# A division moved behind the casts of the weights, and its DMA turn moved behind the last weight load

## The chip, the cores and the metric

One core of a Trainium2 chip. The metric is device time in microseconds (us) of one execution; lower is better. A profile covers one execution; its span is about 1.8 us shorter than that execution's time.

In the lines of the profile PE is TensorE (matmuls), PEld its weight loads, DVE VectorE, ACT ScalarE, POOL GpSimd and SPq the queue of SyncE; L365 is line 365 of the kernel. The granted clock is the share of TensorE's full clock that it was given. A load "lands" when its data is there. The "turn" is the transposing DMA of block 8, the "division" that block's three VectorE instructions (den, reciprocal, multiply).

## The reference

A linear attention with cosine reweighting (batch 8, 8 heads, 576 positions, head size 64) feeds a two-layer network with a gated activation. Cut to what matters:

```python
q_p, k_p = phi(q), phi(k)                  # relu, times cos and sin of the position
kv  = einsum('bhsf,bhsd->bhfd', k_p, v)
num = einsum('bhsf,bhfd->bhsd', q_p, kv)
den = einsum('bhsf,bhf->bhs', q_p, z)[..., None] + 1e-06     # z: sum of k_p over positions
x   = (num / den), heads side by side       # 4608 x 512
h   = x @ w_in                              # 512 x 2048
g   = h * sigmoid(beta * h)
out = g @ w_out                             # 2048 x 512
```

## The kernel before

The 4608 rows of x go through the network in nine chunks of 512 (eight blocks of 64 rows). The first chunk takes blocks 0 to 7 of batch 0; block 8, the last of that batch, is the first of the second chunk. The weights come as float32 through four staging buffers (w_in 0 to 3, then w_out 0 to 3 in the same buffers) and are cast to bfloat16. The order of instructions is written by hand. All the loads below are requested by SyncE, and in the trace of the kernel before they land in the order in which they are requested: raw v, k and q of batch 1 at 33.25, 36.25 and 39.23 us, the turn at 39.70, the halves of w_out 2 at 41.07 and 42.39, those of w_out 3 at 45.19 and 46.54.

```python
def cast_halves(i, fs=(0, 256)):            # each half: 3 casts on VectorE, 1 on GpSimd (i > 1)
    for f in fs:
        for gj in GJ:
            cast_win(i, gj, "pool" if i > 1 and gj == GJ[3] else "dve", f, f + 256)

def rest():                                 # program order behind column tile 4 of the first chunk
    cast_halves(2, (0,))
    x_mul(x_rden(2, 0, 8, NQ, (0, 1)), 8, NQ)      # block 8: den, reciprocal, multiply (VectorE)
    cast_halves(2, (256,))
    cast_halves(3)
    load_w("out", 0); load_w("out", 1)
    load_raw(1, "v"); load_raw(1, "k"); load_raw(1, "q")
    x_turn_dma(0, 8, 9)                            # block 8 turned by a DMA transpose into xt
    load_w("out", 2, 2); load_w("out", 3, 2)
    for j in range(8):
        cast_out(j)                                # w_out 0 and 1, scaled by 1/beta
    v_scale(1, 0); k_relu(1); q_relu(1, 0); q_relu(1, 1)
...
early = {
    4: lambda: (num_mm(8, 0, 2, 0), num_mm(8, 1, 2, 1), rest()),
    ...
    22: lambda: (kv_mm(1, 0, 6), kv_mm(1, 1, 6), kv_take((0, 1), 6, "act")),
    23: second,          # PE transposes q of batch 1; VectorE scales w_out tile 8
}
# slots 4 to 15: h_group(0, slot)              x @ w_in, column tile = slot      (line 365)
# slots 16 to 23: o_part, row tiles 0 to 7 of w_out;  24 to 31: row tiles 8 to 15 (line 390)
# then the second chunk, whose first tile reads block 8
```

## Time and profile before

| | before |
|---|---|
| time | 294.94 us, median of 3 runs (294.49 to 295.12) |
| span, granted clock | 292.5 us, 0.999 |
| PE busy | 285.7 us, 98% |
| part that the change touches | 22 to 51 us |

From the page of the kernel before, the busy tenths of PE and of the DMA engines in 40 slices of 7.3 us:

```profile
PE   8799999999999999999999999999999999999994
...
DMA  7999999999998099807990699139102810131033
```

PE is full nearly everywhere, but so are the DMA engines in nearly all of the first twelve slices.

SyncE's requests in the kernel before (start, length of the request on its queue, line, what):

```profile
24.48 0.51 SPq L78 DMA_DIRECT2D raw_q<-in_q_dram  x1
25.47 5.96 SPq L350 DMA_TRANSPOSE xt<-xs  x1
31.55 4.31 SPq L94 DMA_DIRECT2D w_stage<-in_moe_w_out_dram  x4
```

These are requests, not transfers: raw q, requested at 24.48, lands 14.75 us later, at 39.23. The stretch in which the queue serves the turn shows in the DMA engines' rate (stretch; then busy time and number of instructions of PE, weight loads, VectorE, ScalarE and GpSimd; clock, DMA share, GB/s):

```profile
36.00:37.00 1.00, 1.00 (x7) 0.45 (x5) 0.73 (x1) 1.00 (x3) 0.00 (x0) 1.00 1.05 385
37.00:38.00 1.00, 1.00 (x6) 0.43 (x5) 0.63 (x1) 0.04 (x1) 0.00 (x0) 1.00 1.83 254
38.00:39.00 1.00, 1.00 (x50) 0.68 (x52) 0.00 (x0) 0.00 (x0) 0.00 (x0) 1.00 0.38 80
39.00:40.00 1.00, 1.00 (x43) 0.67 (x32) 0.74 (x2) 0.03 (x1) 0.00 (x0) 1.00 0.94 299
```

### The profile page before, as it was taken

How to read it: one execution, taken by the hardware profiler on the slowest of the kernel's cores; microseconds unless marked ns; L12 is line 12 of the kernel's file. 1: busy time of each engine (PE TensorE's matmuls, PEld its weight loads, DVE VectorE, ACT ScalarE, POOL GpSimd, SP SyncE). 2: the span in 40 equal slices, each digit the busy share in tenths (PEclk: the TensorE clock that was granted, in tenths of full speed). 3: DMA queues.
4: the chain of work that ended last, by engine and by line, in shares of the span. 5: the costliest groups of instructions: out<-in, count | busy, mean ns of one | idle time of the engine just before them, and what ended most of it. 6: DMA issues, size and time to landing. Idle time of an engine off the chain costs nothing.

```text
span 292.5 us, 7217 instructions
## 1 busy us (share of the span) xinstructions
PE 285.7 (98%) x3072; PEld 143.2 (49%) x3072; DVE 114.2 (39%) x287; ACT 143.0 (49%) x228; POOL 74.5 (25%) x89
## 2 busy tenths in 40 slices
PE   8799999999999999999999999999999999999994
PEld 7454455455445544554445444454455444444444
DVE  5989876834900392029301950086005000000000
ACT  5777847862166315721473137412760277137511
POOL 1443000642380038202740255013601210000000
PEclk9999999999999999999999999999999999999999
DMA  7999999999998099807990699139102810131033
GB/s 247 376 391 386 392 312 390 301 249 330 178 284 311 2 173 270 351 6 137 240 394 24 128 235 395 37 67 204 36 2 55 140 36 0 39 83 23 0 74 72
DMA packets 50736, 53.89 MB, mean 184 GB/s; under 512 B 31232, under 2 KB 31632, under 8 KB 50704
## 3 DMA queue, kind: packets, MB, share of 16 engines
q1 hardware_dynamic: 47744, 45.95, 53.7%
q0 software_dynamic: 2688, 7.34, 9.7%
q8 instruction: 24, 0.39, 0.6%
q10 hardware_dynamic: 272, 0.14, 0.2%
q14 instruction: 8, 0.07, 0.1%
HBM read 36.71 MB, written 9.44 MB: 158 GB/s over the span
## 4 chain that ended last, share of the span: by engine, by line
PE 84%; DMA 9%; DVE 4%; issue 0%; SPq 0%
PE ps L390 39%; PE ps L365 38%; DMA w_stage<-in_moe_w_in_dram 4%; PE ps L280 3%; DMA w_stage<-in_moe_w_out_dram 3%; DVE win L108 3%; PE ps L259 2%; DMA raw_q<-in_q_dram 2%; PE ps L408 1%; DVE wout L116 1%; PE ps L339 0%; SPq L78 0%; DVE xs L302 0%; DVE o_sb L411 0%; DVE rden L295 0%
## 5 line engine op out<-in xcount | busy, mean ns | idle before, releaser
L365 PE MATMUL ps<-xt,win 128*128 128x512 bf16 (+1 forms) x580 | 127.7, 378 | 0.2 <-DVE win L108 0.2
L390 PE MATMUL ps<-wout,g_t 128*128 128x512 bf16 x560 | 124.4, 379 | 0.1
L372 ACT ACTIVATE g_t<-ps,beta 128x512 bf16<-128x512 f32 x144 | 98.6, 688 | 33.7 <-PE ps L365 33.7
L365 PEld LDWEIGHTS <-win 128*128 128x128 bf16 x580 | 56.0, 98 | 66.5 <-issue 0.6
L390 PEld LDWEIGHTS <-g_t 128*128 128x128 bf16 x560 | 53.9, 98 | 64.0 <-issue 0.6
L385 POOL DMA_DIRECT2D out_dram<-o_sb x56 | 35.9, 645 | 138.2 <-ACT o_sb L396 138.2
L396 ACT COPY o_sb<-ps 128x512 f32<-128x512 f32 x35 | 20.2, 588 | 98.2 <-PE ps L390 94.0
L271 DVE CAST kv<-ps 128x520 bf16<-128x520 f32 x6 | 4.2, 700 | 68.3 <-PE ps L259 68.3
L217 POOL TENSOR_TENSOR qs<-qt,tanr 128x1152 bf16<-128x1152 bf16 x12 | 28.4, 2384 | 7.0 <-DMA qt<-qb 7.0
L411 DVE COPY o_sb<-ps 128x256 f32<-128x256 f32 (+1 forms) x2 | 0.7, 358 | 62.7 <-PE ps L408 62.7
L302 DVE TENSOR_TENSOR xs<-ps,rden 128x768 bf16<-128x768 f32 (+4 forms) x26 | 22.8, 884 | 0.9 <-DVE rden L295 0.2
L214 DVE TENSOR_SCALAR vb<-raw_v,cos 128x256 bf16<-128x256 f32 x63 | 17.1, 346 | 0.2 <-DMA raw_v<-in_v_dram 0.2
L291 DVE TENSOR_TENSOR den<-ps,eps 128x12 f32<-128x12 f32 (+4 forms) x26 | 4.1, 158 | 33.5 <-PE ps L280 33.5
L214 DVE TENSOR_SCALAR vb<-raw_v,sin 128x256 bf16<-128x256 f32 x54 | 14.7, 345 | 0.0
L280 PEld LDWEIGHTS <-qt 64*64 64x64 bf16 x576 | 10.4, 106 | 4.9 <-issue 4.0
L280 PE MATMUL ps<-kv,qt 64*64 64x65 bf16 x576 | 11.7, 195 | 0.5 <-ACT kv L269 0.5
L189 DVE TENSOR_SCALAR qb<-raw_q 128x1152 bf16<-128x1152 f32 x16 | 11.4, 752 | 1.6 <-DMA raw_q<-in_q_dram 1.6
L280 PE MATMUL ps<-kv,qs 64*64 64x65 bf16 x576 | 11.5, 193 | 0.0
L259 PEld LDWEIGHTS <-rk 64*64 64x64 bf16 x576 | 8.5, 106 | 5.8 <-issue 3.0
L259 PE MATMUL ps<-vb,rk 64*64 64x130 bf16 x576 | 10.2, 218 | 1.0 <-ACT rk L187 1.0
L108 DVE CAST win<-w_stage 64x512 bf16<-64x512 f32 x22 | 10.6, 482 | 1.1 <-DMA w_stage<-in_moe_w_in_dram 0.6
L189 DVE TENSOR_SCALAR rk<-raw_k 128x2304 bf16<-128x2304 f32 (+2 forms) x9 | 10.8, 1199 | 0.6 <-DMA raw_k<-in_k_dram 0.5
(59 smaller groups left out, 101.9 us busy)
## 6 DMA issues: line engine op xcount, KB each, us to landing
raw_v<-in_v_dram SPq DMA_DIRECT2D x7, 1152.0 KB, 9.9
raw_k<-in_k_dram SPq DMA_DIRECT2D x7, 1152.0 KB, 12.3
raw_q<-in_q_dram SPq DMA_DIRECT2D x7, 1152.0 KB, 7.3
out_dram<-o_sb POOLq DMA_DIRECT2D x56, 128.0 KB, 4.1
w_stage<-in_moe_w_in_dram SPq DMA_DIRECT2D x3, 1024.0 KB, 12.9
w_stage<-in_moe_w_out_dram SPq DMA_DIRECT2D x2, 1024.0 KB, 8.1
w_stage<-in_moe_w_out_dram SPq DMA_DIRECT2D x4, 512.0 KB, 11.2
out_dram<-o_sb SPq DMA_DIRECT2D x14, 128.0 KB, 2.3
```

Of the source, the lines that this page charges most:

```text
L108: nc.vector.tensor_copy(o, a)
L189: nc.vector.tensor_scalar(dst, src, scalar1=0.0, scalar2=None, op0=ALU.max)
L214: nc.vector.tensor_scalar(o, a, scalar1=t[:, n : n + 1], scalar2=None, op0=ALU.mult)
L217: eng.tensor_tensor(dst.rearrange("q n (g p) -> q n g p", g=2), src.rearrange("q n (g p) -> q n g p", g=2), tanr[:, n0:n1].unsqueeze(2).to ...
L259: nc.tensor.matmul(t[jj * HP : (jj + 1) * HP, g], lhsT=rk[hs, n, 2 * jp + jj, :], rhs=vb[hs, n, 2 * jp + jj].rearrange("q s e -> q (s e)") ...
L280: nc.tensor.matmul(ps[cols, bank + jj, slot * E : (slot + 1) * E], lhsT=(qt, qs)[cs][rows, jp, n, cols], rhs=kv[rows, g, jp, cs, :], start ...
L302: nc.vector.tensor_tensor(o.rearrange("q j n s d -> q j (n s) d"), nv[:, :, a:z, :, 0:D].rearrange("q j n s d -> q j (n s) d"), rden[:, :, ...
L365: nc.tensor.matmul(ps[:, h_bank(c, jt), blocks.start * 64 : blocks.stop * 64], lhsT=win[jt // 4][:, mi, (jt % 4) * P : (jt % 4 + 1) * P], ...
L372: nc.scalar.activation(g_t, ps[:, h_bank(c, jt)], AF.Silu, scale=beta[:, jt : jt + 1])
L385: eng.dma_start(out=out_v[bb, n][:, m0:m1], in_=o_sb[hf * HP : (hf + 1) * HP, m0:m1])
L390: nc.tensor.matmul(o_ps, lhsT=gs[c, jt][:, tt * P : (tt + 1) * P], rhs=wout[jt // 4][:, jt % 4, :], start=(jt == 0), stop=(jt == JT - 1))
L396: nc.scalar.copy(o_sb, o_ps)
```

## The change

The division no longer stands in front of casts that PE waits for, and the turn no longer stands in front of w_out loads that VectorE waits for. What the division and the turn make is needed only at the start of the second chunk, at 50.7 us.

```diff
     def rest():
-        cast_halves(2, (0,))
+        cast_halves(2)
+        cast_halves(3)
         x_mul(x_rden(2, 0, 8, NQ, (0, 1)), 8, NQ)
-        cast_halves(2, (256,))
-        cast_halves(3)
         load_w("out", 0)
         load_w("out", 1)
         load_raw(1, "v")
         load_raw(1, "k")
         load_raw(1, "q")
-        x_turn_dma(0, 8, 9)
         load_w("out", 2, 2)
         load_w("out", 3, 2)
+        x_turn_dma(0, 8, 9)
```

## The prediction

> **What bounds the kernel now.** I read the page first, then the list of waits of PE, then the chain of waits, then PE's, VectorE's and SyncE's timelines from 16 to 52 us, which is the only part that the change touches.
>
> ```profile
> span 292.5 us, 7217 instructions
> PE 285.7 (98%) x3072; PEld 143.2 (49%) x3072; DVE 114.2 (39%) x287; ACT 143.0 (49%) x228; POOL 74.5 (25%) x89
> ```
>
> PE is busy for 98% of the span, and its mean granted clock is 0.999. A reader should take from this that whatever VectorE or the DMA queue saves is worth nothing unless a wait of PE goes. The list of PE's waits is short; the whole list for the span is:
>
> ```profile
> PE ps L259 <- ACT rk L187: 1.0, 1, 1.0
> PE ps L417 <- DVE zero_b L145: 1.0, 1, 1.0
> PE ps L280 <- ACT kv L269: 0.5, 1, 0.5
> PE ps L365 <- DVE win L108: 0.2, 1, 0.2
> ```
>
> The first three lie in the first 15 us, ahead of everything that the change moves. The last one is PE waiting for a cast of w_in, and that one is in reach. PE's timeline from 26.5 us on shows where:
>
> ```profile
> 26.30 0.77 PE L365 MATMUL ps<-xt,win 128*128 128x512 bf16 x2
> 27.23 5.12 PE L365 MATMUL ps<-xt,win 128*128 128x512 bf16 x23 [0.15 <-DVE win L108]
> 32.19 6.21 PE L390 MATMUL ps<-wout,g_t 128*128 128x512 bf16 x28
> 38.33 1.22 PE L259 MATMUL ps<-vb,rk 64*64 64x130 bf16 x72
> 39.47 1.04 PE L390 MATMUL ps<-wout,g_t 128*128 128x512 bf16 x4
> 40.35 1.17 PE L229 MATMUL ps<-ident,qb 128*128 128x128 bf16 x18
> ```
>
> The columns are start, length, engine, line, operation and count. Undisturbed, 64 such matmuls take 13.81 us in the chain of waits late in the span, 0.216 us each. Between 26.30 and 27.23 only two start: 0.93 us for 0.43 us of work, so **0.50 us** is lost, more than the 0.15 that the idle column shows, because part of it hides in the weight load and in the modelled ends. The 20 matmuls before are column tiles 5 to 9, so the two are the first of tile 10, the first tile that needs the second half of w_in 2. From 27.23 PE runs without a break to 38.33.
>
> The chain of waits in the same stretch shows what is ahead of that cast on VectorE:
>
> ```profile
> 24.61 0.17 DVE den L291
> 24.78 0.02 issue
> 24.81 0.19 DVE rden L295
> 25.00 0.02 issue
> 25.02 0.42 DVE xs L302
> 25.45 0.75 DVE win L108
> 26.19 0.01 issue
> 26.21 0.42 DVE win L108
> 26.63 0.03 issue
> 26.66 0.42 DVE win L108
> ```
>
> This is the division of block 8 (three instructions, from 24.61 to 25.45: **0.84 us**) and then the three casts whose last, ending at 27.08, releases the matmul at 27.23.
>
> One more stretch matters, further down the same chain:
>
> ```profile
> 31.55 9.52 DMA w_stage<-in_moe_w_out_dram
> 41.07 0.03 issue
> 41.10 0.50 DVE wout L116
> 41.60 0.04 issue
> 41.64 1.89 PE ps L390 x8
> ```
>
> In the trace, the last of the transposes before it starts at 41.30, so a matmul could have followed at about 41.43 (other such passages take 0.13); it starts at 41.64, after the scaling of the first w_out 2 tile. Some **0.21 us** is lost there to the landing of w_out 2. These two places, 0.71 us together, are all of PE's loss that the change can reach.
>
> [...] casts alone take 0.42 us, those beside GpSimd's two casts at 22.03 take 0.74 and 0.72, and the first after the division, beside GpSimd's second cast of w_in 3 at 25.30, takes 0.83; the division itself[...] runs beside the first at 24.74 and doesn't wait. [...] while the turn is served, the DMA row between 37.35 and 39.3 us falls from about 390 to between 36 and 207 GB/s but for one slice.
>
> **The change part by part.**
>
> Part 1, the division leaves its place. It takes 0.84 us away ahead of the second half of w_in 2, which now starts at 24.61. But it also exposes these casts to both of GpSimd's casts of w_in 3 in place of one: by the pair at 22.03, each collision costs 0.30 to 0.32 us. So 24.61 + 3 x 0.443 + 2 x 0.31 = 26.56 for the third cast, against 27.08: 0.52 us earlier, not 0.84. PE gets to tile 10 at 26.30 + 0.22 = 26.52 and needs the third cast for its second matmul, at 26.73. So that wait should vanish, with some 0.15 us to spare less the weight load: gain 0.50, or 0.4 if the weight load is late. Then w_in 3: six casts by 0.443 end at about 29.2; its halves are needed by PE at 26.52 + 8 x 0.216 = 28.25 (done 27.9, and the first matmul needs only two of the three) and at 29.97. No new wait.
>
> Part 2, the division comes after them: 29.2 + 0.84 = 30.05. The eight scalings of w_out 0 and 1 follow by 0.40 each and begin at 30.05 in place of 29.79, the price of the second collision. PE now needs the first at 32.19 - 0.49 = 31.70, and one more each 0.216; they end at 30.5, 30.9, 31.35 and 31.75. No wait. All eight are done at 33.3, just when raw v of batch 1 lands (33.25), so the rest of VectorE's row is tied to landings as before: raw k at 36.25 and its relu to 37.63. PE gets to that product at 38.33 - 0.49 = 37.84. Still no wait, with 0.2 us to spare.
>
> Part 3, the early gain meets a landing. VectorE's row goes on:
>
> ```profile
> 36.27 1.36 DVE L189 TENSOR_SCALAR rk<-raw_k 128x2304 bf16<-128x2304 f32 x1 [0.54 <-DMA raw_k<-in_k_dram]
> 39.26 1.43 DVE L189 TENSOR_SCALAR qb<-raw_q 128x1152 bf16<-128x1152 f32 x2 [1.62 <-DMA raw_q<-in_q_dram]
> ```
>
> The loads of v, k and q are requested before the turn in both kernels and land 3.0 us apart (33.25, 36.25, 39.23), which is the pace of the slowest DMA engine, not of the turn. So I leave q at 39.23. Its two relus end at 40.02 and 40.69. PE would be at the transposes at 40.35 - 0.49 = 39.86, has to wait to 40.07 for the first nine, and to 40.74 for the second nine; the last of these starts at 41.17, and the next matmul could start at 41.30.
>
> Part 4, the turn behind w_out 3. On the slowest engine, the turn landed 0.47 us after q (39.70) and w_out 2 1.37 us after that. Without the turn, w_out 2's first half lands at about 40.6. VectorE is free at 40.65, scales its first tile to 41.13, and PE does not wait for it: 41.30 holds, against 41.64. The later halves of w_out come earlier by the same 0.47. SyncE's turn, which took 5.96 us to issue[...], will be issued from about 30.1 on and again hold SyncE for some 6 us; but the requests ahead of it are then in the queue, so DMA does not run dry. The turn lands behind w_out 3, at 46.5 to 48, and is read by PE at 50.35. No wait.
>
> Sum: 0.50 of the first wait, of which 0.21 is paid back to q's landing, and w_out 2's wait (0.21) ends with it; PE at the matmul at 41.64 is early by 41.64 - 41.30 = **0.34 us**. After that PE has no wait to the end, so the gain is carried whole: 294.94 - 0.34 = 294.6.
>
> **The rivals.** First, q's landing (or the relu behind it) takes the place of the whole gain: if the other DMA engines, now busy with w_out 2 while the slowest one still brings q, slow it by 0.3 us, nothing is left: 294.9. For it: its packets took 0.09 us while the others stood still and 0.10 otherwise, so 0.1 us is likely, 0.3 not. Second, the turn was in truth slowing q: then q lands at about 38 to 39, both waits vanish, and the gain is 0.71: 294.2. For it: DMA's throughput fell during q's tail; against it, the even 3.0 us between landings. Third, the turn comes late: if its stall sits at 46 us and its landing slips past 50.35, PE stands for it; each us late is a us: 295.5 or more. Against it: more than 2 us to spare. Fourth, GpSimd's collisions cost more, say three of them: the third cast ends at 26.9, and the first gain falls to 0.3, which ends at the same 294.6, as q decides anyway.
>
> **Range and chances.** All of this is within 0.3% of the time, while the three runs of before are spread by 0.63 us. The first and second rivals bracket 294.2 to 294.9, and the spread of a median adds some 0.2: 294.1 to 295.1. Faster by 2% would need 5.9 us, over eight times what PE loses in reach of the change; slower by 2% would need a stall that nothing here shows. Chances: 0.01 faster, 0.98 within 2%, 0.01 slower.
>
> **What would show it.** In the new profile: PE's wait for the cast of w_in gone, and tile 10 begun at 26.5 with no break; two VectorE casts of over 0.7 us after 24.7 in place of one; the division just before the scalings of w_out, at 29 to 30; q's landing still at 39.2 and a new wait of PE's transposes for the relu of q, 0.2 us; w_out 2's first half landing near 40.6 and the matmul at 41.64 now near 41.3; the dip of the DMA row moved to about 45 us. It would be wrong if PE waited before tile 12, at the first w_out product, or at the first tile of the second chunk for the turn.

The sum came to 41.64 - 41.30 = 0.34 us and so to 294.6. That what is requested later is also served later, which part 4 needs, rests on the order of the landings given with the kernel before.

## The result, and the profile after

The changed kernel took 294.31 us (median of 4 runs, 294.08 to 294.87) against 294.72 (4 runs, 294.36 to 295.12). A ratio is the mean time of one kernel's fast runs over that of the other's of the same rounds, so it is not quite the ratio of the medians: here 0.9989, with a 95% interval of 0.9968 to 1.001. By time alone, that is "the same". The trace says more.

All waits of PE in the profile after (engine, what for; us in total, times, longest):

```profile
PE ps L259 <- ACT rk L187: 1.9, 2, 1.4
PE ps L417 <- DVE zero_b L145: 1.0, 1, 1.0
PE ps L229 <- DVE qb L189: 0.7, 2, 0.5
PE ps L280 <- ACT kv L269: 0.5, 1, 0.5
PE ps L259 <- DVE rk L189: 0.2, 1, 0.2
```

The wait of line 365 for a cast of w_in is gone. The rest of this list says nothing of the change: every wait in it lies before 15 us, the two of line 229 at 5.9 and 7.0 us, where they belong to batch 0. The new wait, of the transposes of batch 1's q for its relu (line 189), stands only in the list of the weight loads, here from 16 to 60 us, first before, then after:

```profile
PEld L365 <- DVE win L108: 0.5, 1, 0.5
```

```profile
PEld L229 <- DVE qb L189: 0.7, 2, 0.5
```

Its two waits lie at 40.29 (0.5 us) and 40.96 (0.2). PE's timeline after:

```profile
25.68 6.42 PE L365 MATMUL ps<-xt,win 128*128 128x512 bf16 x29
31.94 6.21 PE L390 MATMUL ps<-wout,g_t 128*128 128x512 bf16 x28
38.08 1.22 PE L259 MATMUL ps<-vb,rk 64*64 64x130 bf16 x72
39.23 1.04 PE L390 MATMUL ps<-wout,g_t 128*128 128x512 bf16 x4
40.29 1.34 PE L229 MATMUL ps<-ident,qb 128*128 128x128 bf16 x18
```

The 29 matmuls of line 365 run through tile 10 without a break (6.42 us is 29 times 0.216, plus the modelled end of the last). The 18 transposes take 1.34 us in place of 1.17, because the second nine wait for the second relu. VectorE after:

```profile
19.33 10.16 DVE L108 CAST win<-w_stage 64x512 bf16<-64x512 f32 x20 [0.56 <-DMA w_stage<-in_moe_w_in_dram]
29.52 0.16 DVE L291 TENSOR_TENSOR den<-ps,eps 128x4 f32<-128x4 f32 x1
29.71 0.18 DVE L295 RECIPROCAL rden<-den 128x4 f32<-128x4 f32 x1
29.93 0.42 DVE L302 TENSOR_TENSOR xs<-ps,rden 128x256 bf16<-128x256 f32 x1
30.27 3.25 DVE L116 TENSOR_SCALAR wout<-w_stage,rbeta 128x512 bf16<-128x512 f32 x8
...
39.48 1.43 DVE L189 TENSOR_SCALAR qb<-raw_q 128x1152 bf16<-128x1152 f32 x2 [1.65 <-DMA raw_q<-in_q_dram]
40.83 0.49 DVE L116 TENSOR_SCALAR wout<-w_stage,rbeta 128x512 bf16<-128x512 f32 x1
```

All twenty casts stand together, then the division. VectorE still idles for q until 39.48; the first tile of w_out 2 is scaled at 40.83, before PE can use it. The casts that now stand beside GpSimd's two casts of w_in 3 (24.71 to 26.07), each from a narrow window of VectorE's timeline:

```profile
24.84 0.77 DVE L108 CAST win<-w_stage 64x512 bf16<-64x512 f32 x1
```

```profile
25.62 0.74 DVE L108 CAST win<-w_stage 64x512 bf16<-64x512 f32 x1
```

Two casts, not one, are now slowed from 0.42 us beside GpSimd. SyncE's requests after:

```profile
26.87 7.67 SPq L94 DMA_DIRECT2D w_stage<-in_moe_w_out_dram  x4
34.64 2.68 SPq L350 DMA_TRANSPOSE xt<-xs  x1
```

The dip of the DMA engines' rate has moved to where the turn now stands:

```profile
41.00:42.00 1.00, 1.00 (x12) 0.76 (x13) 1.00 (x3) 1.00 (x3) 0.00 (x0) 1.00 1.11 399
42.00:43.00 1.00, 1.00 (x7) 0.39 (x5) 1.00 (x3) 1.00 (x3) 0.00 (x0) 1.00 1.86 307
43.00:44.00 1.00, 1.00 (x59) 0.65 (x58) 1.00 (x3) 0.49 (x2) 0.00 (x0) 1.00 0.88 127
44.00:45.00 1.00, 1.00 (x23) 0.36 (x24) 0.93 (x4) 1.00 (x3) 0.00 (x0) 1.00 0.36 72
45.00:46.00 1.00, 1.00 (x59) 0.68 (x52) 1.00 (x2) 1.00 (x2) 0.00 (x0) 1.00 1.09 347
```

Absolute times of two profiles compare badly here: the run profiled after was 0.24 us late at 22 us, before anything had changed. From the first product of block 8 (line 280) to the first product with w_out 2, the "stretch" below, PE took 41.64 - 21.94 = 19.70 us before and 41.48 - 22.18 = 19.30 after: 0.40 us less. From the first tile of the second chunk to the end both take 241.86 us within 0.02, so in these two profiles what is gained by 50 us is carried to the end. In the other profiles (turn_late aside) this part, in which no kernel differs, took 241.63 to 242.19 us: that spread alone is larger than the gain, which is one reason why the times hardly show it. The kernel before was profiled only once, so its 19.70 has no repetition.

### The profile page after: what moved, and what is told of

Its sections match the earlier page's. It is cut to its first block, busy times and chain, and to the rows that moved or that the text cites. A ratio compares the mean times of both kernels' runs of the same rounds, so it can differ in the third digit from the quotient of the medians.

```text
span 292.4 us, 7218 instructions
## 1 busy us (share of the span) xinstructions
PE 284.0 (97%) x3072; PEld 141.3 (48%) x3072; DVE 114.0 (39%) x287; ACT 142.8 (49%) x228; POOL 74.9 (26%) x89
## 4 chain that ended last, share of the span: by engine, by line
PE 92%; DMA 3%; DVE 2%; SPq 1%; issue 1%
PE ps L365 42%; PE ps L390 42%; PE ps L280 3%; DMA raw_v<-in_v_dram 3%; PE ps L259 3%; PE ps L408 1%; SPq L78 1%; DVE xs L302 1%; PE ps L229 0%; PE ps L339 0%; DVE win L108 0%; DVE rden L295 0%; DVE den L291 0%; DVE rk L189 0%; DVE vb L204 0%
```

## The experiments

Eleven of the twelve were timed in three to five rounds, each on one chip; every output was correct. Three calls of four runs: the medians of the kernel before in them were 294.38, 294.65 and 294.68 us. For each run I took three moments from the trace: **A**, the first product of block 8 on PE; **B**, the landing of raw q of batch 1; and **C**, the first product with w_out 2. The stretch is C - A.

| run | median us | ratio to before, 95% | A | B | wait for a cast | C | stretch | C - B |
|---|---|---|---|---|---|---|---|---|
| before | 294.72 | 1 | 21.94 | 39.23 | 0.49 | 41.64 | 19.70 | 2.41 |
| changed | 294.31 | 0.9989 (0.9968 to 1.001) | 22.18 | 39.45 | - | 41.48 | 19.30 | 2.03 |
| after_again | 293.79 | 0.9977 (0.9964 to 0.999) | 21.73 | 39.06 | - | 41.08 | 19.35 | 2.02 |
| after_third | 294.30 | 0.999 (0.9977 to 1.0002) | 22.52 | 39.40 | - | 41.45 | 18.93 | 2.05 |
| division_only | 295.01 | 1.0013 (1.0001 to 1.0025) | 22.76 | 39.99 | 0.06 | 42.38 | 19.62 | 2.39 |
| division_again | 294.55 | 0.9995 (0.9976 to 1.0014) | 21.97 | 39.02 | - | 41.39 | 19.42 | 2.37 |
| turn_only | 294.43 | 1.001 (0.9984 to 1.0036) | 21.98 | 38.91 | 0.27 | 41.18 | 19.20 | 2.27 |
| division_mid | 294.00 | 0.9979 (0.9966 to 0.9992) | 22.09 | 38.93 | 0.29 | 41.30 | 19.21 | 2.37 |
| early_q | 293.40 | 0.9977 (0.9954 to 0.9999) | 21.81 | 39.32 | - | 40.78 | 18.97 | 1.46 |
| early_q_again | 293.83 | 0.997 (0.9952 to 0.9988) | 21.56 | 38.99 | - | 40.50 | 18.94 | 1.51 |
| early_q_third | 294.10 | 0.9981 (0.9966 to 0.9996) | 21.86 | 39.30 | - | 40.79 | 18.93 | 1.49 |
| turn_early_q | 294.33 | 1.001 (0.9965 to 1.0055) | 21.79 | 39.73 | 0.82 | 41.53 | 19.74 | 1.80 |
| division_early_q | 294.02 | 0.9981 (0.9968 to 0.9994) | 21.61 | 39.48 | - | 41.04 | 19.42 | 1.56 |
| turn_late | 299.35 | 1.0159 (1.0127 to 1.019) | 22.16 | 39.53 | - | 41.56 | 19.40 | 2.03 |

(In the runs with "early_q" q lands in two halves, and B is the second. The wait is what two starts of matmuls at tile 10 or 12 lie further apart than 0.216 us.)

### after_again and after_third: the changed kernel once more

No edit.

> The changed kernel once more, to narrow the interval. I count PE's stretch from the first product of block 8 (21.94 us before, 22.18 after) to the first product with w_out 2 (41.64 before, 41.48 after): 19.70 us before, 19.30 after. Theory (the waits for the cast and for w_out 2 are gone, the relu of q takes 0.33 us back): 19.3 again, and a time 0.3 to 0.5 us under the kernel before, a ratio of 0.9985 to 0.999. Rival (what was measured is noise): ratio 0.9997 to 1.0003 and a stretch that differs from 19.30 by more than 0.1.

Measured: ratio 0.9977, a gain larger than the theory's 0.9985 to 0.999; stretch 19.35, as expected. The rival falls in this series: the interval, 0.9964 to 0.999, excludes 1. The chain that ended last, in this run, names what binds now (start, length, what):

```profile
24.00 15.06 DMA raw_q<-in_q_dram
39.06 0.02 issue
39.08 0.77 DVE qb L189
39.85 0.05 issue
39.90 1.34 PE ps L229 x18
```

From the landing of raw q the chain goes through its relu straight to PE. In the kernel before it went from w_out 2's landing through its scaling.

> The changed kernel beside early_q on one chip, to compare the two. Theory: 0.2 to 0.8 us under the kernel before (ratio 0.9973 to 0.9993), PE's stretch 19.3 to 19.4, and the first product with w_out 2 begins 2.02 us after the landing of raw q, as in both of its profiled runs (2.03 and 2.02; the kernel before 2.41). Rival: no gain, ratio 0.9995 or more.

Measured: ratio 0.999, C - B 2.05, as expected, but a stretch of 18.93 in place of 19.3 to 19.4. In this run PE was late (A at 22.52) while q landed as usual, so PE found the relu done. The stretch alone is therefore no measure of the change; this miss and that of turn_only led to the account after the experiments. The interval of time, 0.9977 to 1.0002, does not exclude the rival of this run (0.9995 or more). Over all, the changed kernel's ratio was under 1 in each of its three series, and one interval of the three excludes 1.

### division_only and division_again: the division moves, the turn stays

```diff
-        load_w("out", 2, 2)
-        load_w("out", 3, 2)
         x_turn_dma(0, 8, 9)
+        load_w("out", 2, 2)
+        load_w("out", 3, 2)
```
(against the changed kernel)

> Only the division moves behind the casts; the turn stays ahead of w_out 2 in SyncE's queue. Theory: the wait for the cast goes (0.5 us), PE then waits for the relu of q (0.3), and w_out 2 lands 1.8 us after q as before, so that the first product with w_out 2 waits for its scaling: stretch 19.65 to 19.75, ratio 0.9995 to 1.0005, nothing gained. Rival (each part brings its share, the cast's 0.5 less the relu's 0.3): stretch about 19.5. Second rival (the turn, now requested behind the later division, holds SyncE so long that w_out 2 is late): stretch over 20.

Measured: stretch 19.62, a little under what the theory asked, and C - B 2.39. The chain:

```profile
32.45 9.37 DMA w_stage<-in_moe_w_out_dram
41.81 0.03 issue
41.84 0.50 DVE wout L116
42.34 0.04 issue
42.38 0.81 PE ps L390 x3
```

The wait for the cast is gone but for 0.06 us, yet PE stands for w_out 2, which lands 1.82 us after q (41.81 against 39.99) with the turn between them. The division alone gains nothing where w_out 2 binds. But the time, ratio 1.0013, was worse than expected, and in the profiled run everything was late from the 13th us on.

> The same kernel as division_only, which came out 0.5 us above the kernel before although nothing of PE's stretch explains it: in its profiled run raw v and all that follows landed 0.6 to 0.8 us late from the 13th us on, before any instruction that differs. Measured against the landing of raw q, the end came 253.25 us later (before 253.32, changed 252.92 and 252.94). Theory (a late DMA stream by chance of the run): ratio back at 0.9995 to 1.0005 and the end 253.2 to 253.3 us after q. Rival (it belongs to this program): ratio over 1.001 again and raw v again landing near 13.0.

Measured: ratio 0.9995, and raw v at its usual place. C - B is 2.37, as where w_out 2 binds; the stretch of 19.42 taken alone would have favoured the first rival of division_only (about 19.5), since q landed earlier after A here. The end came 253.46 us after q, 0.16 later than expected; the difference lies behind the first tile of the second chunk (242.04 us to the end in place of 241.86), where the kernels don't differ. So the slow series did not repeat. Why a stream of the same loads is at times 0.8 us late by 13 us is open.

### turn_only: the turn moves, the division stays

```diff
-        x_turn_dma(0, 8, 9)
         load_w("out", 2, 2)
         load_w("out", 3, 2)
+        x_turn_dma(0, 8, 9)
```
(against the kernel before)

> Only the turn moves behind w_out 3; the division stays between the casts. Theory: the wait at tile 10 stays (0.5 us), so PE is late enough to find q's relu done, and w_out 2 lands 0.4 us earlier: stretch 19.5, a gain of 0.2, ratio 0.9993. Rival (the whole gain is the DMA order's): stretch 19.3. Rival (it is the division's): 19.7.

Measured: stretch 19.20, under every expectation, the rival's too. One run of six, at 296.81, makes its interval of time wide. The trace explains the stretch: q landed only 16.93 us after A here, against 17.29 in the kernel before, so neither q nor w_out 2 bound PE, and the wait for the cast was 0.27 in place of 0.49. 19.20 is 18.93 and that wait. The wait is shorter although the division stands where it stood: the cast after the division took 0.64 us here, against 0.83 in the kernel before. The experiment is a miss as designed: it did not show the part of the turn.

### early_q, early_q_again, early_q_third: the relu of q freed

```diff
-        load_raw(1, "q")
+        load_raw(1, "q", 0, 2)
+        load_raw(1, "q", 2, 4)
-        load_w("out", 2, 2)
+        load_w("out", 2, 1)
```
(against the changed kernel)

> The changed kernel with raw q of batch 1 loaded in two halves, so that its first relu can begin 1.5 us earlier, and w_out 2 in single tiles, so that its first tile lands 0.66 us earlier. Theory (after the change it is the relu of q and nothing else that PE waits for there, 0.33 us): both waits go, stretch 18.95 to 19.05, time 0.3 us under the changed kernel, ratio to before about 0.9977. Rival (something else holds PE as well, such as the scaling of w_out 2 or kv): stretch 19.15 to 19.3, with another name in the list of waits.

> The same kernel as early_q, whose interval was wide for one run at 295.55. Theory: PE's stretch 18.9 to 19.05 again, no wait for the relu of q, ratio 0.996 to 0.9975, below the changed kernel's 0.9977 of the rounds before. Rival (nothing beyond the changed kernel): ratio 0.9975 to 0.9985.

> early_q beside the changed kernel. Theory (it saves the 0.33 us of q's relu): stretch 18.95 and a median 0.2 to 0.5 us under the changed kernel's in the same rounds. Rival (the saved wait is given back later): same median, though the stretch is shorter.

Measured: stretch 18.97, 18.94 and 18.93, with no wait for q's relu in any of the three. VectorE of early_q_third:

```profile
37.82 0.76 DVE L189 TENSOR_SCALAR qb<-raw_q 128x1152 bf16<-128x1152 f32 x1
39.32 0.76 DVE L189 TENSOR_SCALAR qb<-raw_q 128x1152 bf16<-128x1152 f32 x1 [0.74 <-DMA raw_q<-in_q_dram]
40.00 0.49 DVE L116 TENSOR_SCALAR wout<-w_stage,rbeta 128x512 bf16<-128x512 f32 x1
```

and PE there:

```profile
39.78 1.17 PE L229 MATMUL ps<-ident,qb 128*128 128x128 bf16 x18
40.79 0.81 PE L390 MATMUL ps<-wout,g_t 128*128 128x512 bf16 x3
```

The first relu starts 1.5 us before the second, and PE's 18 transposes are back at 1.17 us. The edit changes two things, q's halves and the single tiles of w_out 2, and no run has one without the other. That the relu was what bound is read from the list of the weight loads, where its wait is gone; but in the changed kernel the first tile of w_out 2 was scaled only by 41.32, 0.16 us before PE took it, so q's halves alone would have gained less. All three intervals of time exclude 1, so this version beats the kernel before. Whether it beats the changed kernel, the times do not settle: in the same rounds the medians were 293.40 against 293.79, and 294.10 against 294.30, in the expected direction, with ratios to before of 0.9977 against 0.9977, and 0.9981 against 0.999. The third run's rival, that the time is given back later, is not settled by them either.

### turn_early_q and division_early_q: each part again, with q out of the way

The first is early_q with the division back between the casts of w_in 2; the second is early_q with the turn back ahead of w_out 2.

> early_q with the division back between the casts of w_in 2; the turn stays behind w_out 3. Theory (the division's place is worth its wait at tile 10 only once q no longer binds): the wait of 0.3 to 0.5 us at tile 10 is back and nothing absorbs it, stretch 19.25 to 19.5, 0.3 to 0.5 us slower than early_q. Rival (the division's place is worth nothing anyway): stretch 18.97 as in early_q.

> early_q with the turn back ahead of w_out 2. Theory (the turn's place is worth what it delays w_out 2 by): no wait for the relu of q, but w_out 2's first tile lands 1.15 us after the second half of q in place of 0.68, and the first product with it waits for its scaling by 0.2 to 0.3 us: stretch 19.15 to 19.3. Rival (the turn's place is worth nothing): 18.95.

Measured: without the division's move the wait at tile 10 is 0.82 us, more than expected, and nothing absorbs it: stretch 19.74, 0.80 over early_q of the same rounds. Part of that size is chance: the last w_in landing came later against PE in this run (GpSimd's casts, which wait for it, began at 25.39, 3.60 us after A, against 2.80 in the kernel before), so both of them, 25.39 to 26.98, stood beside the casts of the second half of w_in 2, from 25.34 on. Without the turn's move the stretch is 19.42, 0.49 over early_q_third, more than the 0.2 to 0.3 expected. Of that, 0.32 is a wait for k's relu, which the other runs don't have: the loads lay late against PE in this run (k landed 14.78 us after A, against 14.43 in early_q_third). Behind it PE still stood 0.18 us for the first tile of w_out 2, which landed 0.99 us after q, with the turn between them, against 0.68 in early_q_third. So inside the trace both parts are worth something once q's relu does not bind: in these single profiles 0.8 us for the division, and 0.2 for the turn. The times add little: without the division's move the median is 294.33 against 293.83, with an interval (0.9965 to 1.0055) widened by one execution of 298.16; without the turn's move it is 294.02 against 294.10, so the turn's part does not show in time.

### division_mid: the division between w_in 2 and w_in 3

```diff
         cast_halves(2)
-        cast_halves(3)
         x_mul(x_rden(2, 0, 8, NQ, (0, 1)), 8, NQ)
+        cast_halves(3)
```
(against the changed kernel)

> The changed kernel with the division between the casts of w_in 2 and those of w_in 3. Theory: a wait of 0.3 to 0.5 us comes at tile 12, the first of w_in 3, but q's relu absorbs most of it: the first product with w_out 2 still begins 2.0 to 2.15 us after q lands, and the time is that of the changed kernel within 0.15 us. Rival (a wait of PE always costs its own length): 2.4 us after q, 0.4 us slower than the changed kernel.

Measured: the wait at tile 12 came, 0.29 us, a little under the range. C - B is 2.37, as the rival has it, but not for the rival's reason: q landed early in this run (16.84 us after A), so q had nothing to absorb. The time, 294.00, is 0.3 under the changed kernel's in the same rounds, which only says how little 0.3 us shows in times. Absorption was not shown by this run.

### turn_late: the turn behind the loads of batch 2

```diff
         load_w("out", 3, 2)
-        x_turn_dma(0, 8, 9)
...
             for name in "qvk":
                 load_raw(2, name)
+            x_turn_dma(0, 8, 9)
```
(against the changed kernel)

> The changed kernel with the turn requested still later, behind the loads of q, v and k of batch 2. Theory (the turn is served in its place in the queue, and only its place keeps it free of cost): it lands at about 56.5 us, PE stands at the first tile of the second chunk from 50.5 to about 56.5, time about 6 us longer, ratio 1.02. Rival (turns overtake loads in the DMA engines): it lands near 46, nothing changes.

Measured: 299.35 us, ratio 1.0159, about 5 us over the changed kernel. The turn landed at 54.13, 0.27 us behind raw k (53.86), so the turn kept its place in the queue; it came 2.4 us before the time I had expected, since raw k itself came earlier than in the changed kernel (53.86 against 56.20), where the turn is served ahead of it. The 1.8 us of the queue which the closing list counts for the turn in the changed kernel are most of that. PE's wait and, from the windows view, its clock behind it:

```profile
54.17 1.85 PE L365 MATMUL ps<-xt,win 128*128 128x512 bf16 x4 [3.40 <-DMA xt<-xs]
```

```profile
54.00:55.00 1.00, 0.83 (x3) 0.30 (x4) 0.00 (x0) 0.00 (x0) 1.00 (x3) 0.63 0.91 291
55.00:56.00 1.00, 1.00 (x7) 0.16 (x9) 0.00 (x0) 0.00 (x0) 0.38 (x1) 0.50 0.80 234
56.00:57.00 1.00, 1.00 (x35) 0.65 (x35) 0.23 (x2) 0.69 (x1) 0.00 (x0) 0.50 0.71 262
57.00:58.00 1.00, 1.00 (x5) 0.39 (x4) 0.96 (x3) 0.00 (x0) 0.00 (x0) 0.67 0.08 21
```

The stall is only 3.6 us (50.53 in the changed kernel against 54.17), but after it the granted clock (the third figure from the right) reads 0.63, 0.50, 0.50 and 0.67 in four slices of 1 us, and from there to the end the run takes 243.43 us in place of 241.86: 1.57 us more. In the trace's record the clock is 0.50 for 3.41 us, from 54.25 to 57.66, right behind the 3.40 us for which PE was idle. This is one idle window in one run; what a shorter or longer one does was not tried.

### The account that the runs fit

Two things run towards C. PE, from A on, needs 18.93 us if it never waits (after_third, early_q_third), plus its wait for casts. The queue, from B on, needs 2.02 us through q's relu and the transposes (after_again), or 2.39 us through the turn, w_out 2 and its scaling where the turn stands ahead (division_only). C is the later of the two:

| run | A + 18.93 + wait | B + 2.02 or 2.39 | C measured |
|---|---|---|---|
| before | 41.36 | **41.62** | 41.64 |
| changed | 41.11 | **41.47** | 41.48 |
| division_again | 40.90 | **41.41** | 41.39 |
| turn_only | **41.18** | 40.93 | 41.18 |
| division_mid | **41.31** | 40.95 | 41.30 |
| turn_late | 41.09 | **41.55** | 41.56 |

These six were not used for the three constants, and each is met within 0.02 us. The wait is itself measured, so the first column only says that PE lost nothing else. Where q is loaded in halves the second column does not apply; the first gives 40.74, 40.49 and 41.54 for early_q, early_q_again and turn_early_q (40.78, 40.50 and 41.53 measured), and division_early_q also needs its wait for k's relu and the 0.18 us for w_out 2. The account was formed after the runs, so it is a fit that these six support, not a forecast. It says why no part adds up alone: which side is later hangs on how far q lands behind A (16.84 to 17.38 us in these runs where q is one load, a spread of half a us that the kernel doesn't set). The division's move takes its wait off the first column (0.27 to 0.82 us where the division stands ahead of casts, by where GpSimd's casts fall beside VectorE's: those of w_in 3 began 2.80 us after A in the kernel before, with a wait of 0.49, and 3.60 after A in turn_early_q, with 0.82), the turn's move 0.37 off the second. By this account, only both together move C wherever q lands.

## Why the prediction was right

The forecast was 294.6 us within 294.1 to 295.1, and 294.31 was measured; 0.34 us less on PE was forecast, and 0.40 (or 0.38, counted from q's landing) came. Its mechanism is the one that the runs show. That the size came so near is partly luck: by the stretch, the other two profiles of the changed kernel lie 0.35 and 0.77 us under the one profile of the kernel before. Its steps, one by one, with the 0.22 to 0.24 us by which the profiled run was late taken into account:

- **The first wait vanishes.** It did. One reading of it was off: the matmul at 26.30 is the last of tile 9, as the prediction's own 26.52 for tile 10 implies. Tile 10 begins at 26.68, 0.17 us late, and its second matmul is late by another 0.33, which is the same loss. The third cast was put at 26.56, and it ended at 26.81, 0.25 later as everything was.
- **The second collision with GpSimd.** Two casts of over 0.7 us were forecast; 0.77 and 0.74 were measured.
- **The division and the scalings.** Put at 29.2 and 30.05; 29.52 and 30.27 measured. No new wait at tile 12 or the first w_out product, as forecast. k's relu, with 0.2 us to spare, opened no gap beyond the usual one: the weight loads of line 259 stand for 0.42 us before as after.
- **q's landing is unmoved and takes part of the gain back.** In the changed kernel q landed 6.02 us after raw v, against 5.98 before. The rival in which the turn had slowed q falls. The pay-back was put at 0.21 for the first nine transposes, and the times given for the second nine (40.74 in place of 40.55) imply 0.19 more; 0.19 and 0.18 were measured, by the starts of the single matmuls. The sum in words leaves the second out, but its end, 41.64 less 41.30, has it. early_q shows the pay-back by taking it away.
- **w_out 2 lands earlier, so that C comes at 41.30.** The first half was put at 40.6 and landed at 40.81; C was 41.48, or 41.24 without the lateness. The 0.06 us that C is early comes from one size: the step from the last transpose to the next matmul was put at 0.13 us, and it takes 0.06 where nothing waits (41.42 to 41.48 after), so that w_out 2 had cost 0.28, not 0.21, and 0.78 us, not 0.71, was in reach. So 0.49 less 0.19 and 0.18, plus 0.28, is 0.40. The part of w_out 2 is shown from the other side by division_only, where it stands as before.
- **The turn lands in time.** It did, but at 45.41, not at 46.5 to 48. The step "The later halves of w_out come earlier by the same 0.47" was mis-sized: w_out 3's halves came 1.7 and 1.4 us earlier (43.48 and 45.13 against 45.19 and 46.54). The turn had delayed the DMA engines far more on the mean than the slowest one, from which the 0.47 was read; the closing list has what the packets show. It had no consequence. Nor had a reading of the DMA row: its low slices run from 37.5 to 39.45, not from 37.35 to 39.3.
- **SyncE.** That the turn "will be issued from about 30.1 on and again hold SyncE for some 6 us" was wrong in its place: the four w_out requests held SyncE for 7.67 us, and the turn from 34.64 for 2.68. The longest request here is in both profiles the first behind five loads that had not landed (w_out 0 and 1, raw v, k and q), whichever it is: 5.96 us for the turn before, 3.25 for the first w_out request after. Why it is long was not shown. The queue didn't run dry: from 36 to 42 us the slices of the changed kernel stand at 381 to 399 GB/s.

What the prediction did not see is that the size of the gain is not a property of PE's stretch: in one run in three of the changed kernel q bound nothing, and the gain came from the other column.

## What to carry to other kernels

Where an engine is busy for 98% of the span, look for the few places where it stands, and for each ask what binds next once the wait is gone: here a cast, a weight load and the landing of q lay within 0.5 us of each other, and moving one alone gained nothing that could be shown. A transfer that nobody needs soon belongs behind those that somebody waits for, though not beyond its own need, as the 5 us of the turn that came too late show. A list of waits over the whole span has to be placed in time before it is read: here its largest changes lay where nothing had been changed. Differences below run-to-run noise are to be read from intervals inside the trace, counted from more than one start.

## What the traces show of the turn, the queue and the loads

- The turn is small (128 x 256 elements of two bytes, 64 KB) and stands among loads that run at 390 GB/s. The rates of the four us from 42 to 46 in the changed kernel are 307, 127, 72 and 347: 0.85 MB in place of 1.56, a loss worth 1.8 us of the queue. The dip moved with the turn; before, it lay from 37 to 40 us (254, 80 and 299).
- The packet records of the traces (no view lists them singly) show what this turn did to the loads behind it. The turn is 256 packets of 256 bytes, 18 ns each, against 99 ns for the 2304 bytes of a packet of raw q: 14 GB/s in place of 23 while a packet runs. In the changed kernel 16 packets of the loads behind the turn (as many as there are DMA engines) begin from 42.46 to 44.67 us and all end from 44.92 to 45.03, after the turn's last packet at 44.81. In the kernel before 14 begin from 37.21 to 38.66 and end from 39.13 to 39.17, after its last at 38.98. What they took beyond the usual 0.1 us each is, spread over 16 engines, 1.6 us after and 1.2 before.
- Single requests held SyncE for long: with five loads of about 1 MB ahead of it that had not landed, one took 5.96 us (the turn, before) or 3.25 (the first w_out request, after), against 0.37 to 0.51 for the five requests just before it.
- The stream of loads differed from run to run: with the same instructions up to that point, the second half of raw v of batch 0 landed at 11.77 to 12.97 us in the fourteen profiles. What makes it is open.
